# A new attention order, quarter products for two token chunks, and another order of the second mixing layer

## The chip, the cores and the metric

The kernel runs on one core of one Trainium2 chip. The metric is the time of the whole program on the device in microseconds, the median of three runs.

## The reference

Three layers follow each other, all in float32 accuracy.

```python
# 1 attention: batch 2, heads 8, positions 768, head size 64
scores = q @ k.T / sqrt(64) - slope[h] * dist
keep = (key < 8) | ((0 <= row - key) & (row - key < 96))
a = softmax(where(keep, scores, -1e9))
x = (a @ v) with the heads side by side        # 2 x 768 x 512
# 2 first mixing layer: rank 32, 512 -> 2048 -> 512
u = x + transpose(transpose(x) @ U @ V)
x = u + relu(u @ w_ch1) @ w_ch2
# 3 second mixing layer: 512 -> 1024 -> 512
xk, xr = mu * x + (1 - mu) * x_prev            # mu_k, mu_r
out = sigmoid(xr @ w_r) * (relu(xk @ w_k)**2 @ w_v)
```

The 1536 tokens of both batches stand side by side; q and k are drawn wide, and the weights of both mixing layers arrive as float64.

## The kernel before

A float32 product is made of three passes of TensorE: every operand is kept as a high and a low part, and `PASS` lists high x high, high x low and low x high. So each of the six weight products costs three matmuls for each tile of 128 rows of the inner dimension. The sum of attention and mixing stays in SBUF as `yp` (128 features by four groups kk, by 1536 tokens and a zero column for each batch).

**Attention.** A pair is two heads of one batch; there are eight pairs. TensorE makes the scores `s` (L463), VectorE subtracts the table and finds the row extreme (L471), ScalarE takes the exponential with its sum (L479), VectorE the reciprocal (L484, L485), GpSimd scales (L491), TensorE transposes `P` (L498), ScalarE or VectorE copies the result to `PT` (L724, L726), TensorE multiplies with the values (`xa`, `xb`, L513 and L524), and a copy brings them to `yp`. What of the first mixing layer can be done for batch 0 is put between these steps: the transposes `xtp` with copies `xt`, the rank-32 product (`gps`, `hps`, L823, added to `yp` at L828), the split of the tokens into high and low (`us`, L859 to L868), the conversion of the first weights, and the first product of token chunk 0.

The order of this part is found by the planner `Flow`. Each step has a kind; `COST` gives for each kind the engine, its hold and its latency, and some kinds may go to either of two engines. `Flow.run` simulates the engines and always issues the step that can start first, and of steps that can start within `SLACK` of each other the one of least rank; `BIAS` is added to the rank of a kind, and the calls of `conversion` shift the ranks of the weight rows. A transfer ends when its bytes have passed a queue of `RATE`, `LAND` after its issue. The result is the program's order on each engine.

**First mixing layer.** The 1536 tokens are three chunks c of 512 (chunk 1 spans both batches, in two pieces of 256), the inner size 2048 four blocks g of 512. `m_ch1` makes one tile of the first product (L893, `aps`, 12 matmuls), ScalarE the positive part as its high half (L897), VectorE the low half (L901); four such tiles are `rs`. `m_ch2` makes one tile of the second product (L915, `bps`, 12 matmuls), which VectorE adds to `yp` (L919). A stage of four tiles is 48 matmuls. Results stand in eight banks of PSUM: four with the tag "a" (`s`, `aps`, `kps`, `prs`) and four with "t" (the rest).

**Weights.** Each weight row of 128 x 512 float64 comes by one transfer of 512 KB on SP's queue into `stg` (three buffers) and passes `conv_steps`: `cvt` on VectorE (L655), `c1` on ScalarE (L660), the joins `c2` and `c3` on VectorE (L664, L668), the high part on ScalarE (L672), the low part on GpSimd (L676).

```python
return [("cvt", cvt), ("c1", c1), ("c2", c2), ("c3", c3)] + ([("hi", high), ("lo", low)] if plain is None else [])
```

`queue_weight` puts rows on the list `bgq`, and `st_bg(n)` takes n of them off it beside other work.

**Second mixing layer.** `m_mix` makes the mixed tokens: GpSimd the product with 1 - mu (L1053, `mixt`), VectorE the sum (L1055), ScalarE the high and VectorE the low part (L1057, L1058). `m_k` makes a tile of wk (L1071, `kps`), then ScalarE's positive part (L1075), the square (ScalarE at L1077 in chunk 0, VectorE at L1079 after), the high part on ScalarE (L1080) and the low on GpSimd (L1081). `m_out` makes the gate from wr (L1090, sigmoid at L1094), the product with wv (L1101), the multiplication (L1104) and the output's transfer.

From the first product's chunk 1 on, the order is that of the lists which `weave` merges; each engine runs its instructions in the order written:

```python
weave(st_ch1(0, 2, slot_b) + st_ch2(0, 1), st_bg(6))
weave(st_ch1(1, 0, slot_c) + st_ch2(0, 2), st_bg(2))
```

## Time and profile before

| | us |
|---|---|
| median of the three runs | 519.1 |
| the three runs | 518.87, 519.10, 520.76 |
| the profiled execution | 521.29 |
| its span, first to last instruction | 519.4 |
| TensorE busy | 504.9 |
| VectorE busy | 304.7 |
| ScalarE busy | 217.7 |
| GpSimd busy | 184.1 |

The profiled execution is one run; its span leaves out what lies ahead of the first and behind the last instruction. Its mean granted clock of TensorE is 0.995 of full speed. In the rows of the trace PE is TensorE's matmuls, PEld its weight loads, DVE VectorE, ACT ScalarE, POOL GpSimd and SP the engine whose queue carries the transfers; times are in us unless marked ns.

### The profile page before, as it was taken

The page shows a single profiled execution, that of the slowest core. Times are in us where ns is not written, and L with a number is a line of the kernel's source. Part 1 is how long each engine was busy: PE and PEld are TensorE (multiplying, and loading weights), DVE is VectorE, ACT ScalarE, POOL GpSimd, SP SyncE. Part 2 cuts the span into 40 slices and gives each one's busy share as a digit, 9 for nine tenths or more (in the row PEclk, how much of TensorE's full clock was granted, in tenths as well). Part 3 has the DMA queues.
Part 4 walks back from the last instruction along what each step waited for, and adds up shares of the span by engine and source line. Part 5 has one row for each costly group of instructions (what it writes and reads, how often), then busy time and mean ns, then how long its engine had stood idle before and what let it go on. Part 6 is the DMA issues. An engine that isn't in the chain of part 4 may idle for free.

```text
span 519.4 us, 8649 instructions
## 1 busy us (share of the span) xinstructions
PE 504.9 (97%) x3314; PEld 412.1 (79%) x3314; DVE 304.7 (59%) x672; ACT 217.7 (42%) x508; POOL 184.1 (35%) x247
## 2 busy tenths in 40 slices
PE   8899999989999999999999999999999999999995
PEld 4677688778888888888888888887888888888885
DVE  7899978989982826528265837796043522252110
ACT  6999986455521313214133312444912441144100
POOL 7767784034410404004040403636712442144100
PEclk9999999989999999999999999999999999999999
DMA  8988543313550311304113310031001000100001
GB/s 327 329 286 294 202 137 122 107 65 122 162 187 16 122 40 48 115 0 122 40 25 138 124 39 1 24 138 42 0 21 40 22 0 21 40 21 1 21 21 47
DMA packets 13586, 47.18 MB, mean 91 GB/s; under 512 B 1760, under 2 KB 2144, under 8 KB 13536
## 3 DMA queue, kind: packets, MB, share of 16 engines
q1 hardware_dynamic: 13248, 46.28, 26.4%
q8 instruction: 28, 0.46, 0.4%
q10 hardware_dynamic: 288, 0.26, 0.2%
q14 instruction: 22, 0.18, 0.1%
HBM read 43.39 MB, written 3.15 MB: 90 GB/s over the span
## 4 chain that ended last, share of the span: by engine, by line
PE 81%; DVE 11%; DMA 2%; ACT 2%; issue 1%; POOL 1%; POOLq 0%; SPq 0%; DVEq 0%; ACTq 0%
PE aps L893 26%; PE bps L915 19%; PE pvs L1101 13%; PE kps L1071 11%; PE prs L1090 6%; DVE P L471 3%; PE tp L498 2%; DVE cvc L664 2%; DVE cvc L668 2%; PE s L463 2%; DMA stg<-in_w_dram 1%; PE warm L379 1%; DMA stg<-in_wv_dram 1%; DVE yp L919 1%; PE xa L513 1%
## 5 line engine op out<-in xcount | busy, mean ns | idle before, releaser
L893 PE MATMUL aps<-us,w1s 128*128 128x512 f32 x576 | 135.3, 393 | 0.0
L915 PE MATMUL bps<-rs,w2s 128*128 128x512 f32 x576 | 132.5, 389 | 0.0
L893 PEld LDWEIGHTS aps<-us,w1s 128*128 128x128 f32 x576 | 108.7, 189 | 22.7
L915 PEld LDWEIGHTS bps<-rs,w2s 128*128 128x128 f32 x576 | 108.0, 188 | 23.3 <-PE gps L792 0.8
L897 ACT ACTIVATE rs<-aps 128x512 fp32r<-128x512 f32 x48 | 28.4, 597 | 95.0 <-PE aps L893 94.7
L1071 PE MATMUL kps<-mix,wk 128*128 128x512 f32 x288 | 66.1, 389 | 0.4 <-ACT kf L1075 0.4
L1071 PEld LDWEIGHTS kps<-mix,wk 128*128 128x128 f32 x288 | 54.0, 188 | 12.0 <-ACT kf L1075 0.8
L1101 PE MATMUL pvs<-wv,kh 128*128 128x512 f32 (+1 forms) x208 | 61.9, 373 | 0.0
L901 DVE SCALAR_TENSOR_TENSOR rs<-aps,rs 128x512 fp32r<-128x512 f32 x48 | 32.7, 686 | 41.0 <-ACT rs L897 41.0
L664 DVE SCALAR_TENSOR_TENSOR cvc<-cvc,cvt 128x512 uint32<-128x512 uint32 (+1 forms) x53 | 48.6, 918 | 7.9 <-ACT cvc L660 6.4
L660 ACT ACTIVATE cvc<-stg 128x512 f32<-128x512 f32 (+1 forms) x53 | 35.2, 674 | 41.3 <-DMA stg<-in_w_dram 15.6
L919 DVE TENSOR_TENSOR yp<-bps,yp 128x512 f32<-128x512 f32 (+1 forms) x64 | 33.9, 550 | 25.5 <-PE bps L915 25.4
L491 POOL TENSOR_SCALAR P<-P,sm 128x192 f32<-128x192 f32 x96 | 42.1, 461 | 16.5 <-DVE sm L485 9.6
L1053 POOL TENSOR_SCALAR mixt<-yp,mu 128x512 f32<-128x512 f32 (+1 forms) x32 | 21.6, 682 | 74.1 <-DVE mixf L1055 29.6
L668 DVE SCALAR_TENSOR_TENSOR cvc<-stg,cvc 128x512 uint32<-128x512 uint32 x52 | 45.6, 885 | 0.7
L676 POOL TENSOR_TENSOR w2s<-cvc,w2s 128x512 fp32r<-128x512 f32 x16 | 23.2, 1467 | 63.5 <-ACT w2s L672 63.5
L1101 PEld LDWEIGHTS pvs<-wv,kh 128*128 128x128 f32 x208 | 38.1, 188 | 6.9
L676 POOL TENSOR_TENSOR w1s<-cvc,w1s 128x512 fp32r<-128x512 f32 x16 | 23.9, 1514 | 55.4 <-ACT w1s L672 54.8
L479 ACT ACTIVATE P<-P,nm 128x192 f32<-128x192 f32 x96 | 42.5, 447 | 1.5 <-DVE nm L471 1.4
L1081 POOL TENSOR_TENSOR kl<-kf,kh 128x512 fp32r<-128x512 f32 x24 | 31.0, 1293 | 30.6 <-ACT kh L1080 30.6
L1101 PE MATMUL pvs<-wv,kl 128*128 128x512 f32 (+1 forms) x104 | 38.8, 373 | 0.0
L1055 DVE SCALAR_TENSOR_TENSOR mixf<-yp,mu,mixt 128x512 f32<-128x512 f32 (+1 forms) x32 | 20.3, 653 | 29.8 <-POOL mixt L1053 29.7
(113 smaller groups left out, 589.6 us busy)
## 6 DMA issues: line engine op xcount, KB each, us to landing
stg<-in_w_dram SPq DMA_DIRECT2D x32, 512.0 KB, 4.1
vin<-in_v_dram SPq DMA_DIRECT2D x8, 768.0 KB, 5.6
KK<-in_k_dram SPq DMA_DIRECT2D x7, 768.0 KB, 6.8
stg<-in_wk_dram SPq DMA_DIRECT2D x8, 512.0 KB, 4.2
stg<-in_wv_dram SPq DMA_DIRECT2D x8, 512.0 KB, 4.0
out_dram<-sg SPq DMA_DIRECT2D x11, 256.0 KB, 2.0
QS<-in_q_dram SPq DMA_DIRECT2D x7, 384.0 KB, 5.7
stg<-in_wr_dram SPq DMA_DIRECT2D x4, 512.0 KB, 3.6
```

Of the source, the lines that this page charges most:

```text
L479: nc.scalar.activation(out=Px, in_=Px, func=ACTF.Exp, scale=-1.0, bias=z["nm"][:, i, x:x + 1], accum_out=z["sm"][:, i, x:x + 1])
L491: engine.tensor_scalar(out=Px, in0=Px, scalar1=z["sm"][:, i, x:x + 1], scalar2=1.0, op0=ALU.mult, op1=ALU.mult)
L660: nc.scalar.activation(out=z["c"].bitcast(F32), in_=parts(z)[1].bitcast(F32), func=ACTF.Copy, scale=2.0 ** -112)
L664: nc.vector.scalar_tensor_tensor(out=z["c"], in0=z["c"], scalar=3, in1=z["t"], op0=ALU.logical_shift_left, op1=ALU.bitwise_or)
L668: nc.vector.scalar_tensor_tensor(out=z["c"] if plain is None else plain, in0=parts(z)[1], scalar=0x80000000, in1=z["c"], op0=ALU.bitwise_a ...
L676: engine.tensor_tensor(out=lo, in0=z["c"].bitcast(F32), in1=hi.bitcast(F32), op=ALU.subtract)
L893: nc.tensor.matmul(rs[g, c, f], lhsT=wsl(("w1", g), lw, kk, f * 128, 128), rhs=us[c][:, lx, kk, :], start=(kk == 0 and n == 0), stop=(kk = ...
L901: nc.vector.scalar_tensor_tensor(out=r[:, 1, f, :], in0=rs[g, c, f], scalar=0.0, in1=r[:, 0, f, :].bitcast(F32), op0=ALU.max, op1=ALU.subt ...
L915: nc.tensor.matmul(ps, lhsT=wsl(("w2", g), lw, f, o * 128, 128), rhs=r[:, lx, f, :], start=(n == 0), stop=(n == 11))
L919: nc.vector.tensor_tensor(out=ys, in0=ps[:, a:e], in1=ys, op=ALU.add)
L1071: nc.tensor.matmul(ps, lhsT=wsl("wk", lw, kk, f * 128, 128), rhs=xk[:, lx, kk, :], start=(n == 0), stop=(n == 11))
L1101: nc.tensor.matmul(pv, lhsT=ks[c][lx][:, f, t * 128:(t + 1) * 128], rhs=wsl("wv", lw, f, c0, c1 - c0), start=(n == 0), stop=(n == 23))
```

## The change

Four things change.

- **The planner.** `BIAS` is replaced, `SLACK` is 0.05 in place of 0.02, a transfer counts as landed 1.0 later (`SKEW`), and the shifts of the conversions of the first weights are others.
- **Quarter products.** In blocks 1 to 3 the first product of chunks 1 and 2 is made together. Seen as a product of 2 x 2 quarters (inner rows 0 to 255 and 256 to 511; block columns 0 to 255 and 256 to 511; chunks 1 and 2), it takes eight quarter products; `st_pair` makes it with seven, from sums and differences of quarters. `queue_pair` makes four sums and differences of the weight quarters for each half row pair on VectorE (lines 732 to 735 of the changed file), their high parts on ScalarE and low parts on GpSimd (`w1x`). `diff_raw`, `diff_split` and `diff_late` make those of the tokens once (`diff`; two go into the places of chunk 2's `us` that are no longer needed). A product of `st_pair` is 6 matmuls (line 1021, `pps`); there are 14 in a block, with 14 additions on VectorE (line 1025), 2 copies and 8 positive parts on ScalarE, and 8 subtractions for the low parts on VectorE (line 1029).
- **The order of a block**: the products of chunks 1 and 2, the first product of chunk 0, then the second products of chunks 2, 1 and 0.
- **The second mixing layer**: the weights come in the order wr, wk, wv; every second low part of them is made on VectorE; `mixt` is made on ScalarE; all four gates of a chunk (`m_r`) come ahead of `m_k`, and `m_out` has the product with wv alone.

The diff, cut to what matters here:

```diff
-    BIAS = {"dv": 8, "va": -5, "pt": 2.3, "vps": -3, "vd": -14}
+    BIAS = {"pt": 2, "s": 2, "dk": -17, "dv": -7, "vd": -10, "nm": -16, "sm": -20, "dq": 10, "vps": 5, "y": 7,
+            "hn": -6}
...
-    SWITCH, SLACK, RATE, LAND, LIMIT = 0.13, 0.02, 380.0, 2.4, 2000
+    SWITCH, SLACK, RATE, LAND, LIMIT = 0.13, 0.05, 380.0, 2.4, 2000
+    SKEW = 1.0
...
-                x.end = self.queue
+                x.end = self.queue + self.SKEW
...
-                    for kk in range(kt):
-                        for c0 in range(0, n, 512):
+                    for c0 in range(0, n, 512):
+                        for kk in range(kt):
...
+                            if name in ("wr", "wk", "wv") and kk % 2:
+                                steps[-1] = ("lo", lambda z, f=steps[-1][1]: f(z, "DVE"))
...
+                def queue_pair(g):
+
+                    queue_weight(("w1", g), w1[:, g * 512:(g + 1) * 512], 4, 512, [slot_a("w1s")])
+                    sums[g] = x = slot_a("w1x").rearrange("p (l s k n) -> p l s k n", l=2, s=4, k=2)
+                    rows, bgq[-4:] = bgq[-4:], []
...
+                        def add(_, z=z):
+                            a, b = z[0], z[1]
+                            t = z["t"] = [raw_p.tile([128, 512], F32, tag="raw", name="raw") for _ in range(2)]
+                            s1, s2, s3, s4 = (t[i // 2][:, i % 2 * 256:i % 2 * 256 + 256] for i in range(4))
+                            nc.vector.tensor_tensor(out=s1, in0=a[:, 256:], in1=b[:, 256:], op=ALU.add)
+                            nc.vector.tensor_tensor(out=s3, in0=a[:, :256], in1=a[:, 256:], op=ALU.subtract)
+                            nc.vector.tensor_tensor(out=s2, in0=s1, in1=a[:, :256], op=ALU.subtract)
+                            nc.vector.tensor_tensor(out=s4, in0=b[:, :256], in1=s2, op=ALU.subtract)
...
+                    plus = lambda n: (lambda l, k, j: x[:, l, n - 1, k, j * 128:(j + 1) * 128])
+                    OP = {1: (left[0], lambda l, k: u0[:, l, k, :]), 2: (left[1], lambda l, k: u0[:, l, 2 + k, :]),
+                          3: (plus(4), lambda l, k: u2[:, l, 2 + k, :]), 4: (left[3], lambda l, k: d[:, l, 2, k, :]),
+                          5: (plus(1), lambda l, k: d[:, l, 0, k, :]), 6: (plus(2), lambda l, k: d[:, l, 1, k, :]),
+                          7: (plus(3), lambda l, k: u2[:, l, k, :])}
...
+                    def mm(n, j):
+                        a, b = OP[n]
+                        t = ps[n, j] = bank("at"[n in (1, 2, 3)], "pps")
+                        for k in range(2):
+                            for m, (lw, lx) in enumerate(PASS):
+                                nc.tensor.matmul(t, lhsT=a(lw, k, j), rhs=b(lx, k), start=(k == 0 and m == 0),
+                                                 stop=(k == 1 and m == 2))
...
+                    def relu(r, f, src):
+                        nc.scalar.activation(out=r[:, 0, f, :], in_=src, func=ACTF.Relu)
+                        nc.vector.scalar_tensor_tensor(out=r[:, 1, f, :], in0=src, scalar=0.0, in1=r[:, 0, f, :].bitcast(F32),
+                                                       op0=ALU.max, op1=ALU.subtract)
...
+                    def unit(j):
+                        w0, w1, w2, w3 = w[4 * j:4 * j + 4]
+
+                        def p1():
+                            mm(1, j)
+                            nc.scalar.copy(out=w0, in_=ps[1, j])
+
+                        def p6():
+                            mm(6, j)
+                            add(w1, ps[6, j], w0)
+
+                        def p2():
+                            mm(2, j)
+                            add(w0, ps[2, j], w0)
+                            relu(r0, j, w0)
...
-                        nc.gpsimd.tensor_scalar(out=t[:, a:e], in0=yq, scalar1=mu[:, 2 + which, kk:kk + 1], scalar2=1.0,
...
+                        nc.scalar.activation(out=t[:, a:e], in_=yq, func=ACTF.Copy, scale=mu[:, 2 + which, kk:kk + 1])
...
+                def m_r(c, t):
...
+                    gate[c, t] = tmp_p.tile([128, 512], F32, tag="sg", name="sg", bufs=6)
+                    nc.scalar.activation(out=gate[c, t], in_=pr, func=ACTF.Sigmoid)
...
+                diff_tiles()
+                weave(st_ch1(0, 1, slot_c), [lambda kk=kk: u_split(2, kk, slot_d) for kk in range(4)] + st_diff(0))
+                weave(st_ch1(0, 2, slot_c), st_diff(1) + diff_split(0) + diff_split(1))
+                late_ = [lambda k=k: diff_late(k) for k in range(2)]
+                if G0 == 1:
+                    queue_pair(1)
+                else:
+                    queue_g(1, slot_a, None)
+                weave(st_ch2(0, 1), late_ + st_bg(2))
+                queue_g(1, None, slot_c)
+                weave(st_ch2(0, 2), st_bg(2))
+                for g in range(1, NG):
+                    if g >= G0:
+                        weave(st_pair(g), st_bg(2))
+                    else:
+                        weave(st_ch1(g, 1, slot_b) + st_ch1(g, 2, slot_c), st_bg(2))
+                    if g + 1 < NG:
+                        weave(st_ch1(g, 0, slot_b), st_bg(2))
+                        queue_pair(g + 1)
+                        weave(st_ch2(g, 2) + st_ch2(g, 1), st_bg(4))
+                        queue_g(g + 1, None, slot_c)
+                        weave(st_ch2(g, 0))
                 queue_weight("wr", wr, 4, 512, [slot_a("wr")])
-                queue_weight("wv", wv, 8, 512, [slot_d("wv0"), slot_d("wv1")])
-                weave(st_ch2(3, 2), st_bg(4), st_mix(0, 1, slot_b))
+                queue_weight("wk", wk, 4, DK, [slot_d("wk0"), slot_d("wk1")])
+                weave(st_ch1(3, 0, slot_b), st_bg(4))
+                dctx.close()
+                tmp_p = pool("tmp", 6)
+                queue_weight("wv", wv, 8, 512, [slot_a("wv0"), slot_a("wv1")])
+                weave(st_ch2(3, 0), st_bg(3))
+                weave(st_ch2(3, 1), st_bg(2), st_mix(0, 1, slot_b))
+                weave(st_ch2(3, 2), st_bg(2), st_mix(0, 0, slot_b))
                 for c in range(NCH):
-                    weave([lambda f=f: m_k(c, f) for f in range(8)], st_bg(8))
+                    weave([lambda t=t: m_r(c, t) for t in range(4)], st_bg(4))
+                    weave([lambda f=f: m_k(c, f) for f in range(8)], st_bg(8),
+                          st_mix(c + 1, 1, slot_b) if 0 < c < NCH - 1 else [])
                     weave([lambda t=t: m_out(c, t) for t in range(4)],
-                          st_mix(c + 1, 0, slot_b) if c + 1 < NCH else [])
-                    if c + 1 < NCH:
-                        weave(st_mix(c + 1, 1, slot_b))
+                          (st_mix(1, 1, slot_b) if c == 0 else []) + (st_mix(c + 1, 0, slot_b) if c + 1 < NCH else []))
```

Where instructions move, three places as each engine's program lists them (line, operation, output <- inputs with buffer numbers where rows would read alike, tile, count).

TensorE, block 1: the first product of chunk 1, then the second product, before:

```order
L893 MATMUL aps_2402<-us_1891,w1s_2079 128x512 x12
L893 MATMUL aps_2427<-us_1891,w1s_2079 128x512 x12
L893 MATMUL aps_2442<-us_1891,w1s_2079 128x512 x12
L893 MATMUL aps_2467<-us_1891,w1s_2079 128x512 x12
L915 MATMUL bps_2482<-rs_2262,w2s_2080 128x512 x12
L915 MATMUL bps_2506<-rs_2262,w2s_2080 128x512 x12
L915 MATMUL bps_2520<-rs_2262,w2s_2080 128x512 x12
```

and now, from the end of the second product of chunk 0 and block 0's chunks on:

```order
L950 MATMUL bps_2304<-rs_2092,w2s_85 128x512 x12
L950 MATMUL bps_2338<-rs_2092,w2s_85 128x512 x12
L1021 MATMUL pps_2355<-us_1891,w1s_2169 128x512 x6
L1021 MATMUL pps_2363<-diff_2013,w1x_2170 128x512 x6
L1021 MATMUL pps_2371<-us_1891,w1s_2169 128x512 x6
L1021 MATMUL pps_2381<-diff_2013,w1x_2170 128x512 x6
L1021 MATMUL pps_2399<-us_2014,w1x_2170 128x512 x6
L1021 MATMUL pps_2409<-us_2014,w1x_2170 128x512 x6
L1021 MATMUL pps_2420<-diff_2013,w1s_2169 128x512 x6
```

The whole stages of 12 matmuls a tile have become products of 6, which alternate between weights (`w1s`) and sums of weights (`w1x`).

VectorE, the end of the second product of chunk 0 in block 0: before (L668, L664 and L655 are steps of weight rows, the last row an add of the rank-32 product),

```order
L919 TENSOR_TENSOR yp_63<-bps_1928,yp_63 128x512
L668 SCALAR_TENSOR_TENSOR cvc_2151<-stg_2147,cvc_2151 128x512
L664 SCALAR_TENSOR_TENSOR cvc_2191<-cvc_2191,cvt_2189 128x512
L655 TENSOR_SCALAR cvt_2214<-stg_2212 128x512
L919 TENSOR_TENSOR yp_63<-bps_1942,yp_63 128x512
L668 SCALAR_TENSOR_TENSOR cvc_2191<-stg_2187,cvc_2191 128x512
L655 TENSOR_SCALAR cvt_2239<-stg_2237 128x512
L919 TENSOR_TENSOR yp_63<-bps_1956,yp_63 128x512
L828 TENSOR_TENSOR yp_63<-hps_1970,yp_63 128x256
```

and now (670, 666 and 657 are the same steps):

```order
L954 TENSOR_TENSOR yp_63<-bps_1928,yp_63 128x512
L732 TENSOR_TENSOR raw_2255<-cvc_2224,cvc_2249 128x256
L733 TENSOR_TENSOR raw_2256<-cvc_2224 128x256
L734 TENSOR_TENSOR raw_2255<-raw_2255,cvc_2224 128x256
L670 SCALAR_TENSOR_TENSOR cvc_2284<-stg_2280,cvc_2284 128x512
L954 TENSOR_TENSOR yp_63<-bps_1942,yp_63 128x512
L735 TENSOR_TENSOR raw_2256<-cvc_2249,raw_2255 128x256
L666 SCALAR_TENSOR_TENSOR cvc_2322<-cvc_2322,cvt_2320 128x512
L657 TENSOR_SCALAR cvt_2391<-stg_2389 128x512
L670 SCALAR_TENSOR_TENSOR cvc_2322<-stg_2318,cvc_2322 128x512
L954 TENSOR_TENSOR yp_63<-bps_1956,yp_63 128x512
L863 TENSOR_TENSOR yp_63<-hps_1970,yp_63 128x256
```

Four sums and differences of weight quarters stand among the adds now, and the conversion ahead of the last add is of one row earlier.

TensorE, the last scores of the attention, before

```order
L498 MATMUL tp<-ident,P 128x128 x24
L823 MATMUL hps<-uv 128x256 x2
L463 MATMUL s<-KK,QS 64x192 x8
L513 MATMUL xa<-PT,vin 64x64 x2
L513 MATMUL xb<-PT,vin 64x64 x2
```

and now:

```order
L526 MATMUL xa<-PT,vin 64x64 x2
L526 MATMUL xb<-PT,vin 64x64 x2
L465 MATMUL s<-KK,QS 64x192 x8
L858 MATMUL hps<-uv 128x256 x3
L500 MATMUL tp<-ident,P 128x128 x3
L928 MATMUL aps<-us,w1s 128x512 x3
L500 MATMUL tp<-ident,P 128x128 x15
```

More of the value products stand ahead of the last scores now, and more of the transposes behind them. After them there come 48 matmuls each of `xa` and `xb` where there were 72, and 36 of `tp` where there were 27.

In the whole program `aps` has 288 matmuls in place of 576 and `pps` 252; all other matmuls are as many as before.

## Rows read from the trace of the kernel before

**Rows 1.** The page, part 1: busy us (share of the span) xinstructions.

```profile
PE 504.9 (97%) x3314; PEld 412.1 (79%) x3314; DVE 304.7 (59%) x672; ACT 217.7 (42%) x508; POOL 184.1 (35%) x247
```

**Rows 2.** Chain of waits in order of time: start us, duration us, what.

```profile
240.51 10.88 PE bps L915 x48
251.39 10.88 PE aps L893 x48
```

**Rows 3.** Busy us by stretch, columns in the first row.

```profile
core 0: us, PE busy (x) PEld busy (x) DVE busy (x) ACT busy (x) POOL busy (x), PEclk, DMA share, GB/s
10.00:64.30 54.30, 49.47 (x967) 38.35 (x960) 50.98 (x227) 52.49 (x194) 38.91 (x85) 1.00 0.83 289
64.30:81.20 16.90, 16.89 (x360) 14.38 (x360) 13.80 (x47) 14.05 (x44) 14.15 (x22) 1.00 0.35 112
110.80:349.10 238.30, 238.30 (x1051) 197.26 (x1050) 154.04 (x231) 78.01 (x135) 66.50 (x48) 1.00 0.25 80
```

**Rows 4.** Timeline of TensorE: start us, us, what, count, [idle before, releaser].

```profile
106.68 1.16 PE L823 MATMUL hps<-uv 96*128 96x256 f32 x3 [1.32 <-DVE yp L919]
...
349.15 11.04 PE L1071 MATMUL kps<-mix,wk 128*128 128x512 f32 x48
360.60 1.66 PE L1071 MATMUL kps<-mix,wk 128*128 128x512 f32 x6 [0.41 <-ACT kf L1075]
```

**Rows 5.** Timeline of VectorE, 100 to 107 us.

```profile
100.57 0.69 DVE L919 TENSOR_TENSOR yp<-bps,yp 128x512 f32<-128x512 f32 x1
...
102.38 0.42 DVE L655 TENSOR_SCALAR cvt<-stg 128x512 uint32<-128x512 uint32 x1
102.72 0.68 DVE L919 TENSOR_TENSOR yp<-bps,yp 128x512 f32<-128x512 f32 x1
...
105.60 0.43 DVE L655 TENSOR_SCALAR cvt<-stg 128x512 uint32<-128x512 uint32 x1 [1.60 <-DMA stg<-in_w_dram]
105.94 0.68 DVE L919 TENSOR_TENSOR yp<-bps,yp 128x512 f32<-128x512 f32 x1
```

**Rows 6.** Busy us by stretch, behind the gap (columns as above).

```profile
108.00:112.00 4.00, 4.00 (x12) 3.12 (x11) 3.68 (x8) 1.57 (x5) 0.41 (x1) 0.57 0.00 0
```

**Rows 7.** VectorE's groups by shape: busy us, mean ns of one, idle before.

```profile
L664 DVE SCALAR_TENSOR_TENSOR cvc<-cvc,cvt 128x512 uint32<-128x512 uint32 x52 | 47.9, 922 | 7.9 <-ACT cvc L660 6.4 <-DVE cvt L655 0.5
L901 DVE SCALAR_TENSOR_TENSOR rs<-aps,rs 128x512 fp32r<-128x512 f32 x48 | 32.7, 686 | 41.0 <-ACT rs L897 41.0
...
L655 DVE TENSOR_SCALAR cvt<-stg 128x512 uint32<-128x512 uint32 x52 | 26.3, 507 | 8.5 <-DMA stg<-in_w_dram 4.5 <-DMA stg<-in_wk_dram 2.9 <-DMA stg<-in_wv_dram 0.8
L919 DVE TENSOR_TENSOR yp<-bps,yp 128x512 f32<-128x512 f32 x32 | 22.0, 686 | 21.3 <-PE bps L915 21.2
...
L919 DVE TENSOR_TENSOR yp<-bps,yp 128x256 f32<-128x256 f32 x32 | 11.9, 414 | 4.2 <-PE bps L915 4.2
```

**Rows 8.** Two lines of VectorE alone: ns least/median/most, first and last start.

```profile
L664 DVE SCALAR_TENSOR_TENSOR cvc<-cvc,cvt x53: 673/693/1781, 28.0 to 357.0; 128x512 uint32<-128x512 uint32 x52, 128x384 uint32<-128x384 uint32 x1
...
L901 DVE SCALAR_TENSOR_TENSOR rs<-aps,rs x48: 676/690/694, 86.2 to 328.2; 128x512 fp32r<-128x512 f32 x48
```

**Rows 9.** ScalarE's groups by shape: busy us, mean ns of one.

```profile
L724 ACT COPY PT<-tp 128x384 f32<-128x384 f32 x21 | 9.5, 472 | 0.8 <-PE tp L498 0.6
...
L724 ACT COPY yp<-xa 128x384 f32<-128x384 f32 x7 | 3.3, 468 | 1.3 <-PE xb L524 1.2
...
L724 ACT COPY xt<-xtp 128x512 f32<-128x512 f32 x5 | 2.6, 594 | 0.1
```

**Rows 10.** Timeline of TensorE around the last scores and the first product's end.

```profile
64.31 1.17 PE L498 MATMUL tp<-ident,P 128*128 128x128 f32 x9 [0.25 <-POOL us L862]
...
66.59 0.34 PE L513 MATMUL xa<-PT,vin 128*64 128x64 f32 x4
...
69.72 1.66 PE L893 MATMUL aps<-us,w1s 128*128 128x512 f32 x6
...
81.16 7.78 PE L893 MATMUL aps<-us,w1s 128*128 128x512 f32 x33
```

116 lines of the change are left out of this document (89 added, 27 removed).

## The prediction

> **What bounds the kernel now.** I read the page first: TensorE is busy for 504.9 of 519.4 us, VectorE for 304.7 [rows 1]. A share of 97% is an average, so the chain of waits came next. Through the whole first mixing layer it runs from one group of matmuls to the next: 48 matmuls of the second product, 10.88 us, and after them nothing but the next stage [rows 2]. That is 10.88 / 48 = 0.2267 us for a matmul of 512 columns, the price used below. The busy times by stretch show two regimes [rows 3]. Between 110.8 and 349.1 us TensorE is busy for all of 238.30 us, and VectorE for 154.04: only fewer matmuls shorten this part. Between 10 and 64.3 us ScalarE is busy for 52.49 and VectorE for 50.98 of 54.30 us, TensorE for 49.47: the attention is held by the two vector engines, and the order in which they work sets when it ends. From 64.3 to 81.2 TensorE is full again (16.89 of 16.90).
>
> Last I looked for what TensorE loses between these. There are two places [rows 4]: 1.32 us before the hps matmuls at 106.68, released by VectorE's add at L919, and the first stage of the second layer, where 48 kps matmuls last from 349.15 to 360.60, 11.45 us where 10.88 are due, so 0.57 lost, the end of it waiting for ScalarE's kf. VectorE's own line shows why the first exists [rows 5]: its conversion at L655 stood 1.60 us for a transfer of a weight row, and the add that TensorE wanted (105.94) stood behind it in VectorE's order. Just after that gap the granted clock falls: over 108 to 112 us it is 0.57 on the mean, the lower level, 1.2 GHz instead of 2.4, for most of it [rows 6]; (1 - 0.57) x 4.00 = 1.7 us are lost.
>
> The profiled execution took 521.29 us, 1.89 more than its span and 2.2 more than the median, 519.1. The three timed runs are 518.87, 519.10 and 520.76: the one apart is 1.7 to 1.9 longer, the size of the clock's loss. I take it that the median run does not have that loss, and count the clock only against runs that have it.
>
> **The change, part by part.** *Quarter products.* One block of chunks 1 and 2 took 2 x 48 = 96 matmuls; 14 products of 6 are 84, in all blocks 36 fewer: 36 x 0.2267 = **-8.16 us**. Every matmul left has 512 columns and a weight tile of 128 x 128 as before, so the price stands, and the stretch is TensorE's alone [rows 3], so all of it counts.
>
> What it adds lies on VectorE. In a product stage it runs 14 additions with one operand in PSUM (0.686 us by L919) and 8 subtractions of the kind of L901, with both operands now in SBUF [rows 7]. One follows the other by 0.60 us where VectorE has no wait [rows 5], so these 22 take 13.2 us, and the two weight rows in the same stage, with three steps each, at most 2 x 2.35 = 4.7 (below): 17.9 beside 84 x 0.2267 = 19.04 us of TensorE. Hidden, though not by much. The new differences of weight quarters are 8 additions of 256 columns a block, 0.414 each by L919's short form, 3.3 us. For a whole block: eight weight rows, each a conversion and two joins, at most 0.507 + 2 x 0.922 = 2.35, make 18.8; twelve subtractions at 0.686 make 8.2, the adds to yp 8.8 (eight long, eight short), and now 14 x 0.686 + 3.3 = 12.9 come on top: 48.7 us of 19.04 + 4 x 10.88 = 62.6. Over a block VectorE has room; in the product stage a higher price of one instruction takes it away. ScalarE gets six copies more a block beside a stretch where it is busy for 78.01 of 238.30; GpSimd four subtractions beside 66.50 of 238.30. SP's queue gets no transfer more. The token differences (12 subtractions and their splits) are made once, during block 0, beside plain stages. I cost them at nothing; if their cover went, they would show as a wait of the first product stage, which is the second rival.
>
> Of the two-operand kind the trace shows both prices: L664, two SBUF operands, runs in 0.673 at least and 0.693 us at the median, but 1.781 at most, and 0.922 on the mean; L901, with one operand in PSUM, never leaves 0.676 to 0.694 [rows 7, 8]. If the 8 subtractions took 0.922, a stage of VectorE would be 14 x 0.60 + 8 x 0.922 + 4.7 = 20.5 us, 1.4 more than TensorE's, +4.3 in three blocks if nothing takes the lag up; that end goes into the range. I take 0.60, the lower one, since these stages have little GpSimd work.
>
> [...]
>
> *The gap at 106 us.* In the new order four subtractions of weight quarters stand between the adds, and the conversion that waited for its transfer stands behind the last of them. From the add at 100.57 on, instructions of 512 columns follow each other by 0.60 us and a conversion takes 0.34 [rows 5]; with three quarters at 0.35, the third add starts at 102.8, and with one quarter, a shift, a conversion and a join (0.35 + 0.60 + 0.34 + 0.60) the last ends at about 105.95 where it ended at 106.62. **-0.67 us**; 0.65 of the gap stays. The clock's loss behind it may stay or go: 0, to -1.7 if it goes where a run has it.
>
> *The second layer.* It begins with wr and a sigmoid, one ScalarE instruction to 12 matmuls, where kf took three; the same matmuls otherwise. The four gates hold six buffers of their own. The loss at 360 us goes: **-0.57**. The mixing product moves from GpSimd to ScalarE: 32 instructions at no more than 0.594, the price of a copy of 512 columns from PSUM [rows 9], 19 us spread over the last 160 us, taken as 0; were ScalarE late by them, the loss of 0.57 would stay.
>
> *The attention's new order.* Here the trace cannot be replayed. ScalarE takes, up to the last exponential, seven PT copies more, one yp copy more and two xt copies fewer [rows 9]: 7 x 0.472 + 0.468 - 2 x 0.594 = +2.6 us if ScalarE sets the end. Against it: after the last scores TensorE has one pair's value products less, which ran from 66.59 to 69.72, 3.1 us, and nine transposes more, 1.17 by the row at 64.31 [rows 10]; with the same time of the last scores that is -2.0. I choose 0, between the ends -2.0 and +2.6, since neither engine decides alone.
>
> **Sum:** -8.16 - 0.67 - 0.57 + 0 = -9.4. Against the median 519.1 - 9.4 = **509.7 us**; against the profiled execution, which has the clock's loss and may lose it, 521.29 - 9.4 - 1.7 = 510.2.
>
> **The rivals.** *VectorE becomes the bound in the product stages (slower).* A product holds one bank of four until its addition, so VectorE may lag by two products, 2 x 6 x 0.2267 = 2.7 us, an estimate. This decides where the 22 instructions with the two rows pass 19.04 + 2.7 = 21.7 us, at a mean of (21.7 - 4.7) / 22 = 0.77 us. At 1.0 us they are 26.7, 5.0 over, three times: +15, **524.7**. For it: the maximum of L664; against it: 14 of the 22 have an operand in PSUM, as L901, and never left 0.694. Chance 0.06.
>
> *The products start late.* Each product stage needs the sums of weight quarters, last made by GpSimd. A stall such as the one at 106 us with the slow clock behind it, 1.32 + 1.7, at the head of three stages is +9.1: **518.8**, no change to be told. For it: VectorE's in-order waits [rows 5]; against it: the weights are asked for one stage ahead, 10.88 us or more. Chance 0.08.
>
> *The attention's end moves*, by its bounds: **507.7** or **512.3**. Chance 0.27 for both.
>
> *The clock's loss was in the median run and goes:* **508.0**. Chance 0.10. *Only the products work*, the new lists and the order wr, wk, wv changing nothing of worth: 519.1 - 8.16 = **510.9**. Chance 0.05. That the products are not there is excluded: the order shows 84 in each of three blocks.
>
> **How the numbers follow.** The forecast itself has 0.44. The range: low 509.7 - 1.7 - 2.0 = 506.0; high 509.7 + 4.3 = 514.0, the dearer subtractions, which holds the attention's +2.6 too; outside are the 0.14 of the two costly rivals and a little of combinations. Half a per cent (2.6 us: about what a measurement of this kernel can tell from no change) is 516.5 to 521.7. Faster: all cases but two, 0.86; same: the late start, 0.08; slower: VectorE as bound, 0.06.
>
> **What would show it.** In the changed profile 14 groups of 6 pps matmuls should last 19.04 us with no idle time of TensorE before or in them, and the additions at L1025 near 0.69 us; subtractions at L1029 near 0.69 would bear out the price, near 1.2 or above the first rival. At about 105 us a gap near 0.65 in place of 1.32; at the head of the second layer none. The last of the first aps group should end within 86.8 to 91.4 us, where it ends at 88.9 now [rows 10]. The forecast is wrong if TensorE idles in the product stages, or if the attention ends outside these bounds.

## The result, and the profile after

| | before | changed |
|---|---|---|
| median, us | 519.16 (4 runs, 518.87 to 520.76) | 515.32 (4 runs, 514.30 to 516.13) |
| ratio to before | 1 | 0.9919 (95% interval 0.9892 to 0.9946) |
| profiled execution, us | 521.29 | 515.44 |
| its span, us | 519.4 | 513.7 |
| TensorE, VectorE busy, us | 504.9, 304.7 | 498.3, 358.5 |

The change made the kernel faster by 3.8 us, where 9.4 were forecast; 515.3 lies above the range of 506.0 to 514.0.

The page of the changed kernel, part 1, answers to [rows 1]:

```profile
PE 498.3 (97%) x3278; PEld 405.6 (79%) x3278; DVE 358.5 (70%) x765; ACT 250.2 (49%) x569; POOL 169.0 (33%) x217
```

The timeline of TensorE, in the columns of [rows 4], shows where the changed kernel stands at the places of the forecast, and one place that the forecast does not have:

```profile
94.83 11.22 PE L950 MATMUL bps<-rs,w2s 128*128 128x512 f32 x48
...
107.02 1.17 PE L858 MATMUL hps<-uv 96*128 96x256 f32 x3 [0.61 <-DVE yp L954]
...
152.13 1.52 PE L1021 MATMUL pps<-us,w1s 128*128 128x512 f32 x6
...
171.17 11.04 PE L928 MATMUL aps<-us,w1s 128*128 128x512 f32 x48
...
307.17 2.20 PE L950 MATMUL bps<-rs,w2s 128*128 128x512 f32 x9
310.00 0.51 PE L950 MATMUL bps<-rs,w2s 128*128 128x512 f32 x1 [0.63 <-ACT rs L932]
312.00 32.26 PE L950 MATMUL bps<-rs,w2s 128*128 128x512 f32 x134 [1.50 <-DVE rs L936]
344.10 11.04 PE L1243 MATMUL prs<-wr,mix 128*128 128x512 f32 x48
```

The first second product starts at 94.83, where it started at 93.81 before: the attention ends 1.0 us later. The gap before the hps matmuls is 0.61 in place of 1.32. The first product stage runs from 152.13 to 171.17, 19.04 us for 84 matmuls, and the other two last as long (214.69 to 233.73, 277.25 to 296.29). New is what stands at 307.17. The second product of chunk 0 in block 3 begins, stops after nine matmuls, does one, stops again, and is under way only from 312.00 on. Its three groups of 48 should last 144 x 0.2267 = 32.6 us; from 307.17 to the first prs at 344.10 it is 36.9, so **4.3 us are lost here**: 0.63 + 1.50 of idle time, 1.7 behind it by the clock (next view), and some 0.5 around the two stops.

Busy times by stretch, in the columns of [rows 3]:

```profile
core 0: us, PE busy (x) PEld busy (x) DVE busy (x) ACT busy (x) POOL busy (x), PEclk, DMA share, GB/s
108.00:112.00 4.00, 4.00 (x19) 3.20 (x17) 4.00 (x10) 2.65 (x7) 1.15 (x1) 1.00 0.25 98
152.29:171.33 19.04, 19.04 (x86) 15.77 (x85) 16.58 (x30) 5.76 (x10) 0.00 (x0) 1.00 0.30 96
312.00:316.00 4.00, 4.00 (x11) 3.14 (x12) 3.96 (x6) 2.53 (x4) 1.40 (x1) 0.58 0.47 159
```

The granted clock is now 1.00 over 108 to 112 us, where it was 0.57 [rows 6], and 0.58 over 312 to 316, behind the new wait: (1 - 0.58) x 4.00 = 1.7 us. In both profiled executions the lower level, 1.2 GHz, comes right after TensorE stood still, and in a product stage VectorE is busy for 16.58 of 19.04 us with TensorE full.

Why TensorE waited is read from VectorE's timeline there. L936 makes the low parts of the first product of chunk 0, four of them, one for each tile; the rows begin ahead of the third. L657, L666 and L670 are the conversion and the joins of weight rows of the second layer, L678 their low parts on VectorE:

```profile
304.75 1.52 DVE L657 TENSOR_SCALAR cvt<-stg 128x512 uint32<-128x512 uint32 x1
306.30 0.69 DVE L666 SCALAR_TENSOR_TENSOR cvc<-cvc,cvt 128x512 uint32<-128x512 uint32 x1
306.91 0.68 DVE L678 TENSOR_TENSOR wk<-cvc,wk 128x512 fp32r<-128x512 f32 x1
307.51 0.68 DVE L936 SCALAR_TENSOR_TENSOR rs<-aps,rs 128x512 fp32r<-128x512 f32 x1
308.12 0.68 DVE L670 SCALAR_TENSOR_TENSOR cvc<-stg,cvc 128x512 uint32<-128x512 uint32 x1
308.71 0.42 DVE L657 TENSOR_SCALAR cvt<-stg 128x512 uint32<-128x512 uint32 x1
309.24 0.69 DVE L666 SCALAR_TENSOR_TENSOR cvc<-cvc,cvt 128x512 uint32<-128x512 uint32 x1
309.85 1.50 DVE L657 TENSOR_SCALAR cvt<-stg 128x512 uint32<-128x512 uint32 x1
311.27 0.68 DVE L936 SCALAR_TENSOR_TENSOR rs<-aps,rs 128x512 fp32r<-128x512 f32 x1
```

TensorE has the last of the four tiles done at 307.2. The low part of the third tile starts only at 307.51; that of the last, behind four steps of weight rows, at 311.27, and releases TensorE at 312.00. (ScalarE, which makes the high parts and also waits for VectorE's joins, is late with it: that is the wait of 0.63.) Two of the instructions in the way are conversions that take 1.52 and 1.50 us, where that instruction takes 0.42 at 308.71. GpSimd's timeline over the same stretch has just two instructions:

```profile
304.36 1.63 POOL L678 TENSOR_TENSOR wk<-cvc,wk 128x512 fp32r<-128x512 f32 x1 [5.09 <-ACT wk L674]
309.53 1.54 POOL L678 TENSOR_TENSOR wk<-cvc,wk 128x512 fp32r<-128x512 f32 x1 [3.54 <-ACT wk L674]
```

Each long conversion began while GpSimd made a low part (304.36 to 305.99, 309.53 to 311.07) and ended 0.28 us behind its end. It is so in the whole trace: of the changed kernel's 53 conversions ten took 0.68 to 1.52 us, and each of the ten began while GpSimd made a low part and ended 0.28 or 0.29 behind the low part that it met; one more that began beside a low part (347.08) kept to 0.42, and that low part took 3.16 us. This is what the experiments had to decide: is it the order of the stages (theory A), the number of VectorE's instructions (theory B), or GpSimd standing in VectorE's way (theory C)? And did the planner's new tables cost the 1.0 us at the attention's end?

Of the two prices on which the product stages rested one held throughout and the other at the median, by the view of one line alone:

```profile
L1025 DVE TENSOR_TENSOR sums<-pps,sums x42: 677/690/692, 158.9 to 298.0; 128x512 f32<-128x512 f32 x42
...
L1029 DVE SCALAR_TENSOR_TENSOR rs<-sums,rs x24: 681/684/1774, 161.1 to 300.5; 128x512 fp32r<-128x512 f32 x24
```

The additions keep to 0.677 to 0.692 us, and the subtractions of two SBUF operands to 0.684 at the median, with 1.774 as the worst and 0.827 on the mean: five of the 24 took 0.89 to 1.77 us, and each of the five ran beside a low part on GpSimd. The Trainium skill's rule in "SBUF — State Buffer", section "Who interferes with whom", that an instruction with two SBUF inputs contends with a GpSimd instruction that reads SBUF, agrees: of these two kinds only that one stretches. The same section of the Trainium skill says that single-source instructions such as tensor_scalar can use the port pair that VectorE shares with GpSimd, and then one blocks the other for a whole instruction. The conversion at L657 is of that kind, and 1.50 against 0.42 us agrees. The prediction asked what GpSimd's work does to the new subtractions, and not what it does to the conversions.

### The profile page after: what moved, and what is told of

Its sections match the earlier page's. It is cut to its first block, busy times and chain, and to the rows that moved or that the text cites. A ratio compares the mean times of both kernels' runs of the same rounds, so it can differ in the third digit from the quotient of the medians.

```text
span 513.7 us, 8711 instructions
## 1 busy us (share of the span) xinstructions
PE 498.3 (97%) x3278; PEld 405.6 (79%) x3278; DVE 358.5 (70%) x765; ACT 250.2 (49%) x569; POOL 169.0 (33%) x217
## 4 chain that ended last, share of the span: by engine, by line
PE 83%; DVE 6%; ACT 4%; DMA 2%; POOL 2%; issue 1%; SPq 0%; DVEq 0%; POOLq 0%
PE bps L950 23%; PE pvs L1258 13%; PE kps L1223 13%; PE pps L1021 11%; PE aps L928 10%; PE prs L1243 6%; ACT P L481 2%; PE tp L500 2%; PE s L465 2%; POOL P L493 2%; DMA KK<-in_k_dram 1%; DVE cvc L666 1%; DVE P L473 1%; DVE cvt L657 1%; DMA stg<-in_w_dram 1%
## 5 line engine op out<-in xcount | busy, mean ns | idle before, releaser
L928 PE MATMUL aps<-us,w1s 128*128 128x512 f32 x288 | 67.7, 391 | 0.0
L1233 POOL TENSOR_TENSOR kl<-kf,kh 128x512 fp32r<-128x512 f32 x24 | 31.5, 1313 | 99.3 <-ACT kh L1232 99.3
L928 PEld LDWEIGHTS aps<-us,w1s 128*128 128x128 f32 x288 | 53.7, 188 | 11.0
L1258 PE MATMUL pvs<-wv,kh 128*128 128x512 f32 (+1 forms) x208 | 60.4, 373 | 0.0
L678 POOL TENSOR_TENSOR w1s<-cvc,w1s 128x512 fp32r<-128x512 f32 x16 | 25.3, 1603 | 79.2 <-ACT w1s L674 44.8
L666 DVE SCALAR_TENSOR_TENSOR cvc<-cvc,cvt 128x512 uint32<-128x512 uint32 (+1 forms) x53 | 46.6, 888 | 1.8 <-ACT cvc L662 0.9
L1231 DVE SCALAR_TENSOR_TENSOR kf<-kps,kf 128x512 f32<-128x512 f32 x16 | 11.0, 688 | 46.0 <-ACT kf L1227 46.0
L670 DVE SCALAR_TENSOR_TENSOR cvc<-stg,cvc 128x512 uint32<-128x512 uint32 x52 | 38.1, 743 | 0.3
L1025 DVE TENSOR_TENSOR sums<-pps,sums 128x512 f32<-128x512 f32 x42 | 28.7, 687 | 12.0 <-PE pps L1021 11.3
L657 DVE TENSOR_SCALAR cvt<-stg 128x512 uint32<-128x512 uint32 (+1 forms) x53 | 30.6, 579 | 7.0 <-DMA stg<-in_w_dram 5.7
L1261 DVE TENSOR_TENSOR sg<-pvs,sg 128x512 f32<-128x512 f32 (+1 forms) x13 | 8.4, 647 | 35.6 <-PE pvs L1258 35.6
L1243 PE MATMUL prs<-wr,mix 128*128 128x512 f32 x144 | 33.1, 389 | 0.0
```

What stands on the lines that cost most here:

```text
L657: nc.vector.tensor_scalar(out=z["t"], in0=parts(z)[0], scalar1=2.0 ** -29, scalar2=7.0, op0=ALU.mult, op1=ALU.min)
L666: nc.vector.scalar_tensor_tensor(out=z["c"], in0=z["c"], scalar=3, in1=z["t"], op0=ALU.logical_shift_left, op1=ALU.bitwise_or)
L670: nc.vector.scalar_tensor_tensor(out=z["c"] if plain is None else plain, in0=parts(z)[1], scalar=0x80000000, in1=z["c"], op0=ALU.bitwise_a ...
L928: nc.tensor.matmul(rs[g, c, f], lhsT=wsl(("w1", g), lw, kk, f * 128, 128), rhs=us[c][:, lx, kk, :], start=(kk == 0 and n == 0), stop=(kk = ...
L1243: nc.tensor.matmul(pr, lhsT=xr[:, lx, kk, t * 128:(t + 1) * 128], rhs=wsl("wr", lw, kk, 0, 512), start=(n == 0), stop=(n == 11))
L1258: nc.tensor.matmul(pv, lhsT=ks[c][lx][:, f, t * 128:(t + 1) * 128], rhs=wsl("wv", lw, f, c0, c1 - c0), start=(n == 0), stop=(n == 23))
```

## The experiments

Times are medians, ratios are to runs of the kernel before on the same chip, with a 95% interval. Differences to the changed kernel are to its 515.32 us; measured again (run 11) it took 516.04, so they hold to some 0.7 us. Edits are against the changed kernel unless said otherwise.

**1. The second product of chunk 1 first, in block 3.**

```diff
-                weave(st_ch2(3, 0), st_bg(3))
-                weave(st_ch2(3, 1), st_bg(2), st_mix(0, 1, slot_b))
-                weave(st_ch2(3, 2), st_bg(2), st_mix(0, 0, slot_b))
+                weave(st_ch2(3, 1), st_bg(3))
+                weave(st_ch2(3, 0), st_bg(2))
+                weave(st_ch2(3, 2), st_bg(2), st_mix(0, 1, slot_b) + st_mix(0, 0, slot_b))
```

> The second product of chunk 1 stands ahead of that of chunk 0 in block 3 (the mixing of chunk 0 moves behind with it); nothing else moves. Theory A (the second product of chunk 0 follows its first product at once, and its last low parts stand in VectorE's order behind weight rows of the second layer): TensorE's idle 2.13 us at 309 to 312 and the slow clock behind them go, the stage from the first second product of block 3 to the first prs lasts 32.6 us in place of 36.9; 2.6 to 4.3 us less than the changed kernel, some 511 to 512.7. Theory B (VectorE has too much work there, whatever the order): the wait only moves, to the second tile group or to the mixing of chunk 0 ahead of the first prs, and the time stays within 1 us of 515.3.

Measured: 512.34 us, ratio 0.9836 (0.9797 to 0.9874). TensorE's timeline:

```profile
307.46 32.80 PE L950 MATMUL bps<-rs,w2s 128*128 128x512 f32 x144
340.10 11.04 PE L1243 MATMUL prs<-wr,mix 128*128 128x512 f32 x48
...
359.64 13.89 PE L1223 MATMUL kps<-mix,wk 128*128 128x512 f32 x60 [0.35 <-ACT sg L1247]
```

The three groups of 48 last 32.64 us, with no wait and no slow clock; VectorE's low part comes as late as before (311.59), but nothing wants it then. A new wait of 0.35 us appears at 359.64, for ScalarE. Theory A holds so far: the loss needs the second product of chunk 0 to follow its first at once.

**2. All low parts of wr, wk, wv on GpSimd.**

```diff
-                            if name in ("wr", "wk", "wv") and kk % 2:
+                            if False:
```

> All low parts of wr, wk and wv are made on GpSimd again, ten instructions of VectorE less, the rest as in the changed kernel. Theory A (succession, with waits for transfers and for ScalarE in front): the idle time before the second product of chunk 0 in block 3 shrinks by the two or three low parts in its way, 1.2 to 1.8 of 2.13 us, but some stays. Theory B (load of VectorE by the low parts): it goes wholly. Theory C (VectorE's conversions stand 1.5 instead of 0.42 us while GpSimd runs its low parts): more work on GpSimd makes it longer, 2.5 us or more.

Measured: 519.61 us, ratio 0.9985 (0.9964 to 1.0006): the whole gain is gone. GpSimd and TensorE:

```profile
297.92 5.15 POOL L678 TENSOR_TENSOR wr<-cvc,wr 128x512 fp32r<-128x512 f32 x3
304.96 2.73 POOL L678 TENSOR_TENSOR wk<-cvc,wk 128x512 fp32r<-128x512 f32 x2 [1.89 <-ACT wk L674]
```

```profile
308.89 1.10 PE L950 MATMUL bps<-rs,w2s 128*128 128x512 f32 x3 [0.27 <-DVE rs L936]
311.23 0.76 PE L950 MATMUL bps<-rs,w2s 128*128 128x512 f32 x2 [1.23 <-DVE rs L936]
313.44 0.79 PE L950 MATMUL bps<-rs,w2s 128*128 128x512 f32 x1 [1.46 <-ACT rs L932]
315.45 32.17 PE L950 MATMUL bps<-rs,w2s 128*128 128x512 f32 x134 [1.21 <-DVE rs L936]
```

Ten instructions less on VectorE, and the waits grow from 2.13 to 0.27 + 1.23 + 1.46 + 1.21 (releaser L936 or its high part on ScalarE) = 4.2 us; the mean granted clock of the execution falls to 0.989. Theory B is out. Theory C expected a longer wait, though not by the instructions that it named: the conversions here are no longer than in the changed kernel (0.917 us at the median between 290 and 320 us, where 1.501 is the median there). What grew stands in VectorE's timeline:

```profile
300.41 1.51 DVE L666 SCALAR_TENSOR_TENSOR cvc<-cvc,cvt 128x512 uint32<-128x512 uint32 x1 [0.19 <-ACT cvc L662]
301.84 1.77 DVE L1029 SCALAR_TENSOR_TENSOR rs<-sums,rs 128x512 fp32r<-128x512 f32 x1
...
305.34 1.20 DVE L657 TENSOR_SCALAR cvt<-stg 128x512 uint32<-128x512 uint32 x1
306.65 1.58 DVE L666 SCALAR_TENSOR_TENSOR cvc<-cvc,cvt 128x512 uint32<-128x512 uint32 x1
...
313.29 1.50 DVE L657 TENSOR_SCALAR cvt<-stg 128x512 uint32<-128x512 uint32 x1
```

Beside GpSimd's low parts the joins and subtractions with two SBUF operands take 1.5 to 1.8 us in place of 0.69 too, so all of VectorE's order comes later.

**3. The planner's tables of the kernel before** (the shifts of the conversions go back to the old ones as well).

```diff
-    BIAS = {"pt": 2, "s": 2, "dk": -17, "dv": -7, "vd": -10, "nm": -16, "sm": -20, "dq": 10, "vps": 5, "y": 7,
-            "hn": -6}
+    BIAS = {"dv": 8, "va": -5, "pt": 2.3, "vps": -3, "vd": -14}
...
-    SWITCH, SLACK, RATE, LAND, LIMIT = 0.13, 0.05, 380.0, 2.4, 2000
-    SKEW = 1.0
+    SWITCH, SLACK, RATE, LAND, LIMIT = 0.13, 0.02, 380.0, 2.4, 2000
+    SKEW = 0.0
...
```

> The planner's ranks, slack, landing and conversion shifts are those of the kernel before, all else as in the changed kernel. If the new order costs at the end of the attention what the traces show (the second product of chunk 0 in block 0 starts at 94.83 instead of 93.81), it starts near 93.8 again and the time is 1.0 us less than that of the changed kernel, about 514.3. Rival: the 1.0 us is another execution's spread, the start stays within 0.3 of 94.8 and the time the same.

Measured: 513.33 us, ratio 0.9861 (0.9822 to 0.9899), 2.0 less than the changed kernel; the first second product starts at 94.0. The direction is as expected; of the size, some part is the slow clock, which this profile does not have (the wait in block 3 is there, 0.65 + 1.50).

**4. No products.**

```diff
-                G0 = 1
+                G0 = 4
```

> Blocks 1 to 3 make chunks 1 and 2 with plain products of 48 matmuls again; the sums of weights and the differences of tokens are still made, and not used. If the products are worth their matmuls and hide their additions, 36 matmuls more at 0.2267 us: 8.2 us more than the changed kernel, about 523.5. Rival: the sums and additions cost something in the changed kernel's stages beyond VectorE's cover, then the difference is under 6 us.

For chunk 2 the plain products read the differences that stand in the place of two of its four token groups, so the output is another; number and shape of the instructions are those of plain products. The sums of weight quarters are still made for blocks 2 and 3, not for block 1. Measured: 523.21 us, ratio 1.0069 (1.0045 to 1.0093), 7.9 more than the changed kernel's 515.32; between the medians of runs with like mean granted clock it is 8.5 (0.996 or 0.997) and 8.8 (0.993 or 0.994). The wait in block 3 is there without the products too:

```profile
316.04 2.43 PE L950 MATMUL bps<-rs,w2s 128*128 128x512 f32 x10
320.42 30.71 PE L950 MATMUL bps<-rs,w2s 128*128 128x512 f32 x134 [1.96 <-DVE rs L936]
```

So the products give about what their matmuls are worth, 8.16 us, and they are not what made the wait. The gap at 106 us is 1.2 here, with a conversion that waits 1.42 us for its transfer ahead of the add; with the sums of block 1's quarters in VectorE's order that wait stands behind the add.

**5. The swap and the old tables together** (the edits of 1 and 3).

> Both edits of the first two runs: the second product of chunk 1 ahead of that of chunk 0 in block 3, and the planner's tables of the kernel before. If the two losses have nothing to do with each other, both go: the first second product of block 0 starts near 93.9, no wait of TensorE in block 3, 0.9 us less than the run with the swap alone, about 511.4 where that gave 512.3. Rival: the planner's tables only shifted the same work, the time stays at 512.3.

Measured: 511.04 us, ratio 0.9824 (0.9809 to 0.9838), 1.3 less than the swap alone. Block 3 and the second layer in TensorE's timeline are without any wait:

```profile
307.33 32.80 PE L949 MATMUL bps<-rs,w2s 128*128 128x512 f32 x144
339.97 11.04 PE L1242 MATMUL prs<-wr,mix 128*128 128x512 f32 x48
350.85 22.12 PE L1222 MATMUL kps<-mix,wk 128*128 128x512 f32 x96
```

In this one profile the attention ended late all the same (95.0); the five runs of each kernel decide, 510.22 to 511.14 here, 511.49 to 512.79 with the swap alone. So the two losses are separate: the old tables give 2.0 us alone, 1.3 on top of the swap, and 1.4 on top of run 7 (run 10); the members of the last two pairs were measured on different chips.

**6. The kernel before with the new tables** (the edit of 3 the other way, in the kernel before).

> The kernel before with the new planner's tables and the later landing alone. If the new order costs by itself, the attention ends about 1 us later than before and the time rises by 1.0, to about 520.5; the wait at 106 us stays near 1.3. Rival: it costs only together with the quarter products' weight rows (they take VectorE's time in the attention's last part), then the time is that of before, 519.4, within 0.3.

Measured: 521.32 us, ratio 1.0032 (1.0020 to 1.0043): 1.7 us slower, by the tables alone, and more than the 1.0 expected; the first second product starts at 95.28 in this profile. The exponentials show it best (count, least/median/most ns, first and last start), here and in the kernel before:

```profile
L480 ACT ACTIVATE P<-P,nm x96: 439/447/467, 6.8 to 73.0; 128x192 f32<-128x192 f32 x96
```

```profile
L479 ACT ACTIVATE P<-P,nm x96: 437/445/470, 7.0 to 70.2; 128x192 f32<-128x192 f32 x96
```

The last one starts at 73.0 instead of 70.2. In the changed kernel it is 72.6:

```profile
L481 ACT ACTIVATE P<-P,nm x96: 437/445/470, 6.8 to 72.6; 128x192 f32<-128x192 f32 x96
```

So ScalarE gets its exponentials done 2.4 to 2.8 us later in these rows, and over the fourteen profiles of this study the last exponential starts at 72.6 to 73.7 with the new tables and at 70.2 to 72.3 with the old, five of those seven at 70.7 or below. Up to it ScalarE makes 21 copies of `PT` with the new tables and 14 with the old, in every profile, which is what the prediction counted for its +2.6. TensorE, with a pair's value products less to do after it, gets part of that back: the first second product starts 1.0 us later in the changed kernel, with the last exponential 2.4 later.

**7. All low parts of wr, wk, wv on VectorE.**

```diff
-                            if name in ("wr", "wk", "wv") and kk % 2:
+                            if name in ("wr", "wk", "wv"):
```

> All low parts of wr, wk and wv on VectorE, none on GpSimd; the rest as in the changed kernel. Theory C (while GpSimd makes a low part, a conversion of VectorE stands up to 1.5 us in place of 0.42, two of them ahead of the last two low parts of block 3's chunk 0): these conversions take 0.42, the idle 2.13 us shrink to under 1 us although VectorE has more instructions; 1.2 to 3 us less than the changed kernel. Theory B (too many instructions on VectorE): each low part more costs 0.6 us there, two or three of them stand ahead, the wait grows to 3 us or more.

Measured: 511.95 us, ratio 0.9846 (0.9830 to 0.9862), 3.4 less than the changed kernel with ten *more* instructions on VectorE. The conversions between 290 and 320 us, in the changed kernel and here:

```profile
L657 DVE TENSOR_SCALAR cvt<-stg x5: 419/1501/1519, 304.8 to 318.3; 128x512 uint32<-128x512 uint32 x5
```

```profile
L657 DVE TENSOR_SCALAR cvt<-stg x4: 423/425/430, 305.1 to 317.5; 128x512 uint32<-128x512 uint32 x4
```

and TensorE in block 3:

```profile
307.95 33.08 PE L950 MATMUL bps<-rs,w2s 128*128 128x512 f32 x144
340.87 11.04 PE L1243 MATMUL prs<-wr,mix 128*128 128x512 f32 x48
```

The median conversion falls from 1.501 to 0.425 us, and the three groups last 32.92 us, 0.28 over their due, though the second product of chunk 0 still follows its first at once. GpSimd has no instruction at all between 294 and 320 us here. Theory C is shown from both sides, with the joins and subtractions of run 2 added to it: more low parts on GpSimd make the wait longer (2), none remove it (7).

**8. The mixing product on GpSimd again** (with the edits of 5).

```diff
-                        nc.scalar.activation(out=t[:, a:e], in_=yq, func=ACTF.Copy, scale=mu[:, 2 + which, kk:kk + 1])
+                        nc.gpsimd.tensor_scalar(out=t[:, a:e], in0=yq, scalar1=mu[:, 2 + which, kk:kk + 1], scalar2=1.0,
...
```

> As the run with both edits, and the mixing product is made on GpSimd again as in the kernel before. If ScalarE's new work is what makes TensorE wait 0.35 us in the first group of kps (360 us in the run with the swap), that wait goes and the time falls by 0.3 to 0.6 us. Rival: GpSimd's instructions lengthen VectorE's of two operands more than ScalarE gains, the mixed tokens of chunk 0 come later and TensorE waits at the first prs or kps for 1 us or more.

Measured: 521.33 us, ratio 1.0020 (1.0003 to 1.0038), 10.3 more than without this edit. TensorE's waits (in all, times, longest, in us):

```profile
PE pvs L1258 <- POOL kl L1233: 4.1, 2, 2.3
PE kps L1223 <- ACT sg L1247: 2.6, 2, 1.5
```

The rival came, and larger than it was put. For 4.1 us TensorE waits for the low parts of k (L1233), which stand behind mixing products in GpSimd's order. For 2.6 it waits for the gates (L1247), which ScalarE reaches late: it waits 2.72 us for a join on VectorE ahead of one, and 1.87 for a weight row's transfer ahead of another. Behind the longest wait, 2.29 us, the granted clock is 0.57 from 440 to 444 us, 1.7 us more; the rest of the 10.3 is not told apart. So the new second layer needs the move of the mixing product to ScalarE, which the prediction took as 0.

**9. All three: swap, low parts on VectorE, old tables** (1, 7 and 3).

> The changed kernel with the swap, with all low parts of wr, wk and wv on VectorE and with the planner's tables of the kernel before. The swap and the low parts cure the same wait, so together they give little more than one: some 510.5 to 511.0, where swap and tables gave 511.0. Rival: with no wait at 309 to cover, ten more instructions on VectorE delay the mixed tokens of chunk 0 and TensorE waits at the first prs or kps; then 512 or more.

Measured: **510.15 us**, ratio 0.9811 (0.9784 to 0.9839), five runs between 509.82 and 510.40, a little under the 510.5 to 511.0 expected. It beats both kernels.

**10. Low parts and tables, without the swap** (7 and 3).

> As the run before it without the swap: the stages of block 3 in the changed kernel's order. Theory C alone (the wait comes from GpSimd's low parts standing in VectorE's way): the second product of chunk 0 may follow its first at once, TensorE waits there for under 0.5 us, and the time is within 0.5 us of the run with all three. Theory A (succession) gives the swap a value of its own of 1 us or more.

Measured: 510.54 us, ratio 0.9816 (0.9788 to 0.9844), the same as run 9 within the intervals. The order of the stages is needed for the wait, as run 1 shows, but with GpSimd out of the way it costs nothing that can be told.

**11. The changed kernel again.**

> The changed kernel itself, beside the others on one chip. 515.3 as before, within 0.7; its profile with the wait of about 2 us in block 3.

Measured: 516.04 us, ratio 0.9915 (0.9886 to 0.9944), 0.7 above the first measurement, with the wait in block 3 at 1.50 + 0.64. Of its ten timed runs in this study, six have a mean granted clock of 0.993 or 0.994 and took 515.44 to 516.99; four have 0.997 and took 514.13 to 515.19. The slow clock behind the wait comes in most runs, not in all.

**12. All low parts of the weights of blocks 1 to 3 on VectorE too** (with the edits of 9).

```diff
-                            if name in ("wr", "wk", "wv") and kk % 2:
+                            if name not in (("w1", 0), ("w2", 0)):
...
-                                nc.gpsimd.tensor_tensor(out=o, in0=t, in1=h.bitcast(F32), op=ALU.subtract)
+                                nc.vector.tensor_tensor(out=o, in0=t, in1=h.bitcast(F32), op=ALU.subtract)
```

> As the run with all three, and the low parts of the weights w1, w2 of blocks 1 to 3 and of the sums of weights are on VectorE too: 12 instructions more a block, 7.2 us of VectorE by 0.60 each, GpSimd idle in the first mixing layer after block 0. If contention with GpSimd had cost VectorE about as much, its conversions keep to 0.42 and 0.69 us, the product stages stay at 19.04 us and the time stays within 0.5 us of the run with all three. Rival: VectorE, which has some 50 of 62.6 us in a block, gets 57 and becomes late in a product stage; then TensorE waits there, 1 us or more in each block.

Measured: 510.15 us, ratio 0.9816 (0.9782 to 0.9850), run 9's time. VectorE's groups (busy us, mean ns of one):

```profile
L665 DVE SCALAR_TENSOR_TENSOR cvc<-cvc,cvt 128x512 uint32<-128x512 uint32 (+1 forms) x53 | 36.4, 693 | 1.2 <-ACT cvc L661 0.7
...
L656 DVE TENSOR_SCALAR cvt<-stg 128x512 uint32<-128x512 uint32 (+1 forms) x53 | 23.4, 446 | 8.6 <-DMA stg<-in_w_dram 4.0 <-DMA stg<-in_wk_dram 3.0 <-DMA stg<-in_wv_dram 1.3
```

The join at L665 takes 0.693 us on the mean, where the shape of 512 columns took 0.879 in run 9 and 0.922 before (L664, [rows 7]); the conversion takes 0.446, where it took 0.506 in run 9 and 0.507 before. Part 1 of the pages, run 9 and this run:

```profile
PE 495.4 (98%) x3278; PEld 404.1 (80%) x3278; DVE 355.6 (70%) x778; ACT 250.1 (49%) x566; POOL 151.1 (30%) x207
PE 495.5 (97%) x3278; PEld 404.2 (80%) x3278; DVE 353.5 (70%) x814; ACT 250.8 (49%) x566; POOL 96.3 (19%) x171
```

With 36 instructions more VectorE is busy for 2.1 us less. Twelve instructions more a block fit under TensorE.

## Why the prediction was wrong, by its own steps

- **Products, -8.16 us: right.** Three stages of 19.04 us; without them (run 4) 7.9 more. The additions kept to their price; the subtractions took 0.827 us on the mean where 0.60 to 0.69 was taken, and the cover was enough all the same: VectorE is busy for 16.58 us of a stage, where 17.9 was reckoned. The first rival, VectorE as the bound of a product stage, did not come; run 12 gave it more instructions and it still kept up.
- **The gap at 106 us, -0.67: right.** 1.32 became 0.61, and where block 1 has no sums of quarters (run 4) it is 1.2 again.
- **The second layer, -0.57: right in the sum**, 169.6 us from its first matmul to the end of the span (513.7 - 344.10), 170.25 before (519.4 - 349.15), so -0.65. The changed kernel's profile has no wait of TensorE there, so the mixing product cost nothing on ScalarE, as taken; on GpSimd it costs 10.3 us (run 8).
- **The attention, 0 between -2.0 and +2.6: mis-sized.** It was +1.0 in the profile (the last of the first aps group ends at 89.96, inside the bounds given), and the tables alone are +1.7 (run 6). ScalarE's +2.6 did come, as a last exponential 2.4 later; of TensorE's -2.0 there came 1.4. Choosing the middle because "neither engine decides alone" was the weak step: the two ends were not alternatives but followed each other.
- **"Over a block VectorE has room": the step that failed.** The 48.7 us of 62.6 are a mean over a block, and the last block is not like the others. There the second product of chunk 0 follows its first at once, without two other second products between, and the weight rows of the second layer come into the same stage. The prediction costed the new block order at nothing and asked of no stage what TensorE wants next and what stands before it on VectorE. What the runs showed in its place is 4.3 us in that stage, 2.13 + 0.5 + 1.7, which go with the swap (run 1) or with the low parts on VectorE (run 7). The rival "the products start late" had this mechanism and nearly the price, a wait behind VectorE's order with the slow clock behind it, 1.32 + 1.7; the place was wrong, and it came once. Neither of the signs by which the prediction would know itself wrong came: TensorE does not idle in the product stages, and the attention ends within its bounds.
- **The price of a conversion** was taken as its mean, 0.507 [rows 7]; where GpSimd makes a low part beside it, it was up to 1.52. The prediction asked for GpSimd's work in the product stages alone, where there is little (0.00 us over 152.29 to 171.33); the stage that mattered was the one behind the third of them.

The account: 509.7 + 1.0 (attention) + 2.6 (wait, with its starts) + 1.7 (slow clock behind it, in most runs) = 515.0, against 515.3 measured. With the wait and the tables' cost taken out the same kernel takes 510.15 us (run 9), against the 509.7 forecast. Between the two profiled executions the clock's 1.7 stands on both sides: 519.4 - 8.16 - 0.71 - 0.65 + 1.02 + 2.6 = 513.5, measured 513.7.

What stays open: which entry of the planner's tables delays the exponentials, since they were only tried together; and why the slow clock follows the wait in some executions and not in others.

## What to carry to other kernels

Room on an engine is to be counted stage by stage, above all in the last round of a loop, where the work of the next phase comes in: for each stage, ask what the bound engine wants first and what stands ahead of that on the engine that makes it. Moving work off a busy engine onto an idle one can lengthen the busy one's other instructions; run both directions (2 and 7) before believing the count of instructions. An idle time of 2 us on a TensorE that is otherwise full cost about twice its length in the profiled execution, by the clock that fell behind it.
